# A third written order for the 791 pieces of an attention-and-experts kernel

## The chip, the cores and the metric

The kernel runs on one core of a Trainium2 chip. The metric is the device time of one execution in microseconds (us), as the median over several runs. The core has five engines that run side by side, each through its own instructions in order: PE (TensorE, matrix multiplication), DVE (VectorE), ACT (ScalarE), POOL (GpSimd) and SP (SyncE, which here only issues DMAs). An instruction that waits for another engine or for a DMA holds up all that stand behind it on its own engine. POOL issues DMAs too: the loads of the experts' weights, the scatters of token rows, and the writes of the output rows.

## The reference

A Nystrom attention over 8 batches of 8 heads (sequence 576, head dimension 64, 32 landmarks) gives 4608 tokens of 512 numbers. A mixture of 8 experts follows: each token goes to the expert with its greatest logit.

```python
q_lm = q.reshape(B, H, m, S // m, D).mean(axis=3)
k_lm = k.reshape(B, H, m, S // m, D).mean(axis=3)
A, Bm, C = sm(q, k_lm), sm(q_lm, k_lm), sm(q_lm, k)
Z = Bm.transpose(0, 1, 3, 2) / (norm_1(Bm) * norm_inf(Bm) + 1e-06)
for _ in range(6):
    Z = 2 * Z - Z @ Bm @ Z
x = rows_of(A @ Z @ C @ v)
...
e_idx = np.argmax(x @ w_gate, axis=1)
for e in range(E):
    mask = e_idx == e
    h = np.maximum(x[mask] @ w1[e], 0.0)
    out[mask] = gate_w[mask, None] * eom[mask, e, None] * (h @ w2[e])
```

`gate_w` is the softmax probability of the chosen expert and `eom` a sigmoid of `x @ w_output_gate`.

## The kernel before

The work is cut into eleven streams, Python generators that put instructions on the engines when they are advanced. A *piece* is what one advance emits, up to the generator's next `yield`. The string `ORDER` (line 20) holds one letter for each advance: line 950 walks along it, and each letter advances its stream by one piece. There are 791 pieces. So the string sets the order of the instructions on every engine at once, and no scheduler moves them afterwards. A stream that isn't ready (an event it needs hasn't been marked) answers "blocked", the letter then does nothing, and what is left at the string's end is done by a loop (line 952) that tries the streams in the order L G M T C A E N O R X. Pieces are numbered from 0 in their stream: X158 is the 159th piece of X.

The attention goes by 16 groups (4 heads of one batch), two to a batch, four to a pair of batches:

- L `loading` (line 752): q, k and v of a group are loaded by SP into parts of the weight buffer that aren't used yet (lines 216 and 220). A load needs that the group two before has used its place.
- G `summing` (line 223): POOL adds up q or k into landmarks, five instructions a piece (lines 228 to 232).
- M `marking` (line 235): ACT scales the landmarks.
- T `turning` (line 242): PE turns q and k, ACT copies them out of PSUM (lines 255, 256). Three pieces make q, three make k.
- C `softmax_c` (line 267) and A `softmax_a` (line 314): scores on PE, softmax on DVE and ACT.
- N `iteration` (line 339): the iteration for Z, eleven pieces a batch. Most are a few small matmuls (line 358) and one DVE instruction that waits for them (line 378), which the next piece waits for in turn.
- O `outputs` (line 403): five pieces a batch, each with eight matmuls (line 421), an ACT copy (425) and a DVE reduction (427). They use one PSUM buffer, the same one as the down projections of stream X.

Then the experts:

- R `directing` (line 838): for each pair of batches `routing` (line 449), which ends with nine scatters by POOL that sort the token rows by expert into `x_sorted` (line 528), and then the tables that say which rows a tile takes. Pair 0 is followed by a ranking of the experts by their token count (line 551). Of R's 73 pieces, R19 completes table 0, R55 to R68 are the routing of pair 3, R69 to R72 the last table (line 609): R70 computes how many tiles the ending has (line 627) and R72 the rows' addresses (line 655). In pair 3 SP also writes eight blocks of zero rows (line 522).
- E `bringing` (line 848): 32 loads, four for each expert, on POOL's queue (lines 141 and 144).
- X `working` (line 872): 26 *static* tiles of 128 rows in three stages. Stage 0 takes 8 tiles of the two largest experts, once table 0 is done; stage 1 takes 10 more, with pair 1's table; stage 2, the free tiles, takes 8 of any of the five largest, with pair 2's table. A tile is fetched by SP (lines 674 and 681; the first five of a stage in its first piece, each later one five tiles ahead), turned (line 695), multiplied up (707 or 718), in stage 2 turned again (726, copied by DVE at 728), and multiplied down (735) in two pieces that hold the output buffer. DVE scales (741) and POOL writes the rows out (743).

X0 is the first fetch of stage 0, X49 of stage 1, X110 of stage 2. In stage 2, X157 turns the hidden rows of the seventh tile (line 726). Piece X158 comes with a condition of its own:

```python
if stage == last - 1 and j == n - 2:
    yield from need("table", last)
    tables["which"] = which_ending()
    tc.switch_hint(tables["which"], len(ENDINGS), label="ending")
```

Every engine there reads the ending's number (`which_ending`, line 868), and X158 goes on with the first half of the last static tile. Behind all pieces stands a switch (line 965) over nine endings of different length. Its tiles are fetched by transposing DMAs (line 678), three ahead, and multiplied with an expert chosen by a register. In the profiled execution 12 tiles ran there.

While the attention runs, X's up projections use the two PSUM buffers of the transposes. When the last scores are done, stream A closes the attention's buffers (line 810), and from then on they have two of their own.

Of the kernel before, what the change touches and what calls it, by code (L numbers as in the profile page):

```python
# [17 lines left out]


ORDER = (  # L20
    "TTTGTTLTMCTGCTTACGCMCATTCTLMATCCTLAAAAGTCALCMTTCTCNGANLMCNATCGTLALCAACTGMCLTTANTLAMNCCTLGCANCNNLTCAN"
    "AANMGTCCTNNLTATAOLGAMCCNLGATOAACCTMAGNOCANTLTACTMNTANCLMNONNCACNLACNGOTTCGTMCANOALONTTATLOCCNOATNCGA"
    "AMNOCTRRCTCNARLRMNRTTTRLARCLNTNGCMNRRLGRRCRARAAACTCNCLTRTNLRNTAGOTLMATNRTEENRCRCONRCRNAGCNONTAMAACCG"
    "AEOTXTATNONLXCAALNCMGATTACCOTCAEAEXXOMXCOOLXTNMATXGAOLLRTRTNXERGLAXCXXMTXCNTRGCACRMTECCTAATNRARXMNCC"
    "XNXXNARRLTCENTAXCEXNXLTACTXLGTXARAALNLRGRETXXCNXMTNGCNAAXXONRXETXCNXNXAOLXANAOTNRAXNACOMNCGXTONCEXML"
    "TNALCRTXAGOCCXLXOTXXAMCXCAXGRETOCAOXXRCOTNNTTTXXERNXERCMNXXRRXXANREETXEXCNXRXARCRNXRRAXEMXEXREAETXXT"
    "CTXNXTRNRCTXRNXXXCLXAXEXCCEXXXXCRNCOXCEAAOAXXACXXXXXNEAXXAXXEXNOEXXEONXXNXXEOANRXXXXRXXNXXXRENXNXANE"
    "XXXXAXNXXXNAXXOXOOXOXXXOXRRRRRXRXXXXRXXRXXXXRRXXXRRRXXXXXXXXXRRXXXXXXRXXXXXXXRRXXXXXXXXXXXX"
)


# [972 lines left out]
```

## Time and profile before

| | us |
|---|---|
| median of 3 runs | 403.58 |
| the runs | 401.46 to 405.55 |
| the profiled execution, whole | 400.38 |
| its span, first to last instruction | 398.8 |
| PE busy | 330.1 |
| PE weight loads busy | 211.4 |
| DVE busy | 224.5 |
| POOL busy | 215.2 |
| ACT busy | 174.1 |

The profile is of one execution. The views used are: the page (busy time of each engine, and its share in 40 slices of the span); the view by windows (busy time in chosen stretches, with the clock granted to PE as a share of the full one, and the DMA engines' mean busy share, which comes out over 1 in some stretches); the view of waits (who waited for whom, in total, times, longest); and the timeline, whose rows give start, duration, engine, line, operation, output and inputs, and in brackets how long the engine idled before it and what ended that. PEld are weight loads, which run beside PE's matmuls. SPq and POOLq are the issuing sides of DMA queues. "issue" is an idle time for which the profile names no releaser. PE's busy time is modelled for pipelined matmuls.

### The profile page before, as it was taken

Reading aid. Unit: us, or ns where it says so; the run is one execution under the profiler, and the core shown is the slowest. Engines: PE = TensorE matmul, PEld = TensorE weight load, DVE = VectorE, ACT = ScalarE, POOL = GpSimd, SP = SyncE. Lnnn points to the kernel's source line nnn. Section 1 sums busy time; section 2 is a strip of 40 time slices with the busy share of each in tenths; the row PEclk is TensorE's granted clock in tenths of the full one; section 3 lists DMA queues with packets and bytes.
Section 4 is the critical chain, followed back from the end, with each engine's and each line's share of the span. In section 5 each row is a group of like instructions: output and inputs, shape, how many; then the busy total and the mean of one; then the engine's idle time right before and its main releaser. Section 6 shows DMA issues by size and latency. Waiting matters only on the chain. (4 is left out here: it accounts for less than half of the span.)

```text
span 398.8 us, 11916 instructions
## 1 busy us (share of the span) xinstructions
PE 330.1 (83%) x4503; PEld 211.4 (53%) x4532; DVE 224.5 (56%) x584; ACT 174.1 (44%) x413; POOL 215.2 (54%) x319
## 2 busy tenths in 40 slices
PE   2987878898679788989898999899989758799981
PEld 1555555665346655755566676576544424355540
DVE  5267776588587498655664844456527354234240
ACT  2565665767327655443555345342242112232320
POOL 2876966375885485488855565753312751022221
PEclk9999999999959999998999999999999989999997
DMA  8755555534748998984693999999940532323311
GB/s 265 225 181 189 172 179 181 129 105 137 265 81 186 292 220 227 172 256 99 136 252 79 221 240 244 211 218 228 255 135 27 200 132 58 97 73 100 96 54 46
DMA packets 46743, 66.44 MB, mean 167 GB/s; under 512 B 16208, under 2 KB 35024, under 8 KB 46672
## 3 DMA queue, kind: packets, MB, share of 16 engines
q0 software_dynamic: 17568, 30.98, 35.4%
q1 hardware_dynamic: 29104, 34.56, 29.8%
q8 instruction: 39, 0.64, 0.6%
q14 instruction: 32, 0.26, 0.2%
HBM read 65.35 MB, written 15.91 MB: 204 GB/s over the span
## 5 line engine op out<-in xcount | busy, mean ns | idle before, releaser
L743 POOL DMA_INDIRECT out_dram<-y,ic x38 | 39.1, 1030 | 102.6 <-DVE y L741 83.0
L735 PE MATMUL py<-W,hT 128*128 (+1 forms) x281 | 70.7, 382 | 6.5 <-DVE hT L728 4.4
L228 POOL TENSOR_TENSOR lms<-W 128x576 f32<-128x576 f32 x30 | 42.9, 1429 | 40.5 <-DMA W<-in_q_dram 39.4
L741 DVE TENSOR_SCALAR y<-py,ic 128x512 f32<-128x512 f32 x38 | 28.5, 750 | 62.5 <-PE py L735 46.2
L255 PE MATMUL tp<-ident,W 128*128 128x128 f32 x288 | 51.6, 301 | 12.7 <-ACT W L256 7.4
L256 ACT COPY W<-tp 128x512 f32<-128x512 f32 (+1 forms) x96 | 48.0, 517 | 29.5 <-PE tp L255 29.0
L721 ACT ACTIVATE h<-ph 128x512 bf16<-128x512 f32 x40 | 23.9, 598 | 64.7 <-PE ph L718 38.8
L735 PEld LDWEIGHTS <-hT 128*128 128x128 bf16 x304 | 29.2, 99 | 37.2 <-DVE hT L728 4.7
L255 PEld LDWEIGHTS tp<-ident,W 128*128 128x128 f32 x288 | 34.9, 150 | 23.3 <-ACT W L256 11.2
L528 POOL DMA_INDIRECT x_sorted<-row,r_slot x36 | 36.6, 1017 | 14.3 <-issue 5.2
L707 PE MATMUL ph<-xT,W 128*128 128x128 bf16 x576 | 38.1, 219 | 1.8 <-issue 1.0
L421 PE MATMUL po<-vbd,AT 64*128 64x160 f32 (+1 forms) x320 | 33.6, 326 | 5.1 <-DVE L L427 4.4
L707 PEld LDWEIGHTS <-W 128*128 128x128 bf16 x576 | 33.3, 98 | 5.8 <-issue 4.6
L427 DVE TENSOR_REDUCE L<-po 128x16 f32<-128x128 f32 (+1 forms) x40 | 11.6, 289 | 43.6 <-ACT row L425 43.6
L710 ACT ACTIVATE hT<-ph 128x512 bf16<-128x512 f32 x36 | 21.3, 597 | 33.5 <-PE ph L707 23.7
L425 ACT CAST row<-po 128x512 bf16<-128x512 f32 (+1 forms) x40 | 23.4, 586 | 24.5 <-PE po L421 20.2
L358 PE MATMUL pw<-WV 32*32 32x96 f32 (+1 forms) x768 | 26.9, 252 | 7.9 <-DVE WV L378 5.8
L264 PE MATMUL S<-W 64*32 64x288 f32 x512 | 27.0, 480 | 5.5 <-ACT BC L289 3.7
L421 PEld LDWEIGHTS po<-vbd,AT 64*128 64x128 f32 (+1 forms) x320 | 22.8, 178 | 13.1 <-DVE L L427 6.4
L229 POOL TENSOR_TENSOR lms<-lms 128x256 f32<-128x256 f32 x30 | 25.2, 839 | 2.4
L358 PEld LDWEIGHTS pw<-WV 32*32 32x32 f32 x768 | 15.9, 108 | 19.3 <-DVE WV L378 10.2
L718 PE MATMUL ph<-W,x 128*128 x95 | 22.4, 379 | 1.7 <-DVE y L741 1.3
(166 smaller groups left out, 539.0 us busy)
## 6 DMA issues: line engine op xcount, KB each, us to landing
W<-in_moe_w_dram POOLq DMA_DIRECT2D x32, 512.0 KB
W<-in_q_dram SPq DMA_DIRECT2D x16, 576.0 KB
W<-in_k_dram SPq DMA_DIRECT2D x16, 576.0 KB
W<-in_v_dram SPq DMA_DIRECT2D x16, 576.0 KB
x<-x_sorted SPq DMA_DIRECT2D x26, 128.0 KB
x_sorted<-zeros SPq DMA_DIRECT2D x9, 129.0 KB
ic<-x_sorted SPq DMA_DIRECT2D x38, 1.0 KB
out_dram<-y,ic POOLq DMA_INDIRECT x38
```

The source lines that it names most:

```text
L228: nc.gpsimd.tensor_tensor(s, t[:, :hg, :], t[:, hg:, :], op=OP.add)
L229: nc.gpsimd.tensor_tensor(s[:, 0:4, :], s[:, 0:4, :], s[:, 4:8, :], op=OP.add)
L255: nc.tensor.transpose(p[:, i, :], in_=tv[:, c0 + i] if c0 + i < hg else lm, identity=I128)
L256: nc.scalar.copy(tT[:, c0:c0 + n, :], p[:, :n, :])
L264: nc.tensor.matmul(p[hs, par, :hg * 32], lhsT=lhs[pr, hg, hs], rhs=cols(rhs[pr, :hg, hs]))
L358: nc.tensor.matmul(p[hs, gi, lo:32 + D], lhsT=cur[hs, gi, :32], rhs=cur[hs, gi, lo:])
L421: nc.tensor.matmul(po[ps, hp, gi * 2 * VC:(gi + 1) * 2 * VC], lhsT=ATs[gi][hs, 128 * c:128 * c + n], rhs=vbd[hs, gi].rearrange("p a b -> p ...
L528: i = nc.gpsimd.indirect_dma_start(out=xs, out_offset=bass.IndirectOffsetOnAxis(ap=slot[:, c:c + 1], axis=0), in_=rows[c], in_offset=None)
L707: nc.tensor.matmul(ph[:, 128 * i:128 * i + 128], lhsT=columns(t, dc * F + (half * FCH // 2 + i) * 128, 128), rhs=t["xT"][:, dc, :], start= ...
L735: nc.tensor.matmul(t["py"], lhsT=t["hT"][:, fc, :], rhs=columns(t, DCH * F + fc * HD, HD), start=(fc == 0), stop=(fc == FCH - 1))
L741: nc.vector.tensor_scalar(out=y, in0=t["py"], scalar1=t["coef"], scalar2=None, op0=OP.mult)
L743: i = nc.gpsimd.indirect_dma_start(out=out, out_offset=bass.IndirectOffsetOnAxis(ap=t["id"], axis=0), in_=y, in_offset=None, bounds_check= ...
```

## The change

Only the string is replaced, by another of 791 letters with the same number of each.

```diff
 ORDER = (
-    "TTTGTTLTMCTGCTTACGCMCATTCTLMATCCTLAAAAGTCALCMTTCTCNGANLMCNATCGTLALCAACTGMCLTTANTLAMNCCTLGCANCNNLTCAN"
+    "TTTTTLTGCCGMTTTMCACTCGTMATCTACTAAALGCCCAMLTTTCATACLLGNCMCTGLLNATAAGLNCATMTCNCCNALGTNMTANCATLCNTCALNA"
...
-    "XXXXAXNXXXNAXXOXOOXOXXXOXRRRRRXRXXXXRXXRXXXXRRXXXRRRXXXXXXXXXRRXXXXXXRXXXXXXXRRXXXXXXXXXXXX"
+    "NOAENXXNOXXXOXXOXXOXORRXXRRXARXRXXXRXXRXXXRXXXXXRRXRXRXXXERXRXXXXXEXXXXXXXXXXXXXRXXXRXXXXRX"
 )
```

Place of some events, counted in pieces from the start of the work:

| event | before | after |
|---|---|---|
| expert 0, 1, 2, 3, 4 fully issued | 331, 411, 496, 566, 590 | 311, 376, 411, 500, 574 |
| expert 5, 6, 7 fully issued | 626, 664, 699 | 665, 691, 766 |
| pair 0, 1, 2, 3 scattered | 255, 480, 612, 761 | 273, 461, 611, 758 |
| table 0, 1, 2, last | 284, 537, 691, 778 | 329, 504, 661, 781 |
| attention over, its buffers closed | 711 | 728 |

In the old string each letter does its piece. In the new one eight letters X near the end find X158 blocked, since the last table isn't done; R70, R71 and R72 then stand directly behind one another after X157, and the last eight pieces of X are done by the closing loop. In the old order R70 stands ahead of X148, and R71 and R72 ahead of X155.

What stands between the nine scatters of a pair on POOL's queue, in the two programs (s a scatter, y a write of output rows, G the five instructions of a landmark sum, E an expert load):

| pair | before | after |
|---|---|---|
| 0 | s s s s s s s s s G | s s G s s s s G s s s G |
| 1 | s s s s G s s E y G s s E y s G | s s s s y s s G s s y E s E G |
| 2 | s s E E s s E E y s s s s s y E E | s s s s s s y s s s y y E y E |
| 3 | s s s s s s s s y s y y y | s s s s y s s s s E s y E y y |

On SP's queue the first fetches of stage 0 stand, in the old order, ahead of v of group 10 and q, k and v of group 11; in the new one behind them. The outputs of pair 3, the routing of it (R55 to R63) and the free tiles keep about the places that they had relative to one another.

More of the change, by code (lines that the diff above doesn't have):

```diff
@@ L20 @@
 ORDER = (
-    "TTTGTTLTMCTGCTTACGCMCATTCTLMATCCTLAAAAGTCALCMTTCTCNGANLMCNATCGTLALCAACTGMCLTTANTLAMNCCTLGCANCNNLTCAN"
[L22 to L27, printed above, removed]
-    "XXXXAXNXXXNAXXOXOOXOXXXOXRRRRRXRXXXXRXXRXXXXRRXXXRRRXXXXXXXXXRRXXXXXXRXXXXXXXRRXXXXXXXXXXXX"
+    "TTTTTLTGCCGMTTTMCACTCGTMATCTACTAAALGCCCAMLTTTCATACLLGNCMCTGLLNATAAGLNCATMTCNCCNALGTNMTANCATLCNTCALNA"
+    "CANMACNTGTCNTTNOLNAMOCALCALANTOACGCTNCMCAGTTANTTMNCCLLLTANGATAOCMTAONCNGATTACGTMACNTLNCOLNCAOLANATCO"
+    "GCAATONACNMAORTTNRCTARGCMLNCTRNTRRAMNRRTRTLCNGCTANCLLRCTGLNALMNCCORNRGTRMRACARAAGTCATTCNRCRTTNCCONAE"
+    "NLECMONRAECECCATLONTNLREATLNORNGANOXMTONTAONXLOTGAXNACAXMXOCLXEXRAETARCXCAXXEMTGARXXARETNCXAXTECEAXT"
+    "TRRXXRXALNXECCXXLMXTRTNTGCRANRMRCNXNRCALXOGXACXTNRTXXAATNMXEXRXNAONCNEXXXCTRCGRXXNAOLTTXCXXAEXXMXCOL"
+    "EGLXRNTXLACNTXXNEMTGTXELXNCXXTCXNOGXXTOCLCOCAEMAATCOXXONXNXAXLNXXXTNAOXRXTEAEXXRCGRXXNRMXXRTERARRRRX"
+    "XCRRTXCMXRNRRCAXAXXTXTATRXAXXCNACXXTXRXCXNXCAXEXXNCCACNXCNXAORXXNEXEXNXNXEAXXXXNXNOXAXNOXNEEXAXENXAO"
+    "NOAENXXNOXXXOXXOXXOXORRXXRRXARXRXXXRXXRXXXRXXXXXRRXRXRXXXERXRXXXXXEXXXXXXXXXXXXXRXXXRXXXXRX"
 )
```

## The prediction

> **What bounds the kernel now.** First the page: how full TensorE is.
>
> ```profile
> span 398.8 us, 11916 instructions
> ## 1 busy us (share of the span) xinstructions
> PE 330.1 (83%) x4503; PEld 211.4 (53%) x4532; DVE 224.5 (56%) x584; ACT 174.1 (44%) x413; POOL 215.2 (54%) x319
> ```
>
> PE is the one full engine, and the change neither adds nor removes an instruction of the computation. So 330.1 us of PE work stay, and only the 68.7 us in which PE idles (398.8 - 330.1), and stretches at half clock, can change. The page's row of PE in tenths has two hollows behind the start, near 105 and 320 us. The view by windows, read next, measures these and two smaller ones like them:
>
> ```profile
> 104.00:110.00 6.00, 2.73 (x49) 1.52 (x34) 2.09 (x11) 1.03 (x4) 4.87 (x9) 1.00 0.53 196
> 110.00:122.00 12.00, 9.42 (x140) 5.98 (x140) 9.28 (x21) 3.16 (x8) 10.01 (x14) 0.57 0.53 96
> 174.00:178.00 4.00, 2.43 (x31) 1.45 (x33) 1.99 (x5) 1.21 (x3) 3.61 (x5) 1.00 0.88 336
> 178.00:184.00 6.00, 5.78 (x71) 3.21 (x64) 3.25 (x10) 1.75 (x5) 5.14 (x9) 0.72 0.13 43
> 248.00:256.00 8.00, 5.90 (x104) 4.23 (x104) 4.08 (x15) 2.98 (x9) 5.23 (x8) 1.00 0.98 244
> 312.00:325.00 13.00, 7.39 (x43) 3.45 (x43) 4.77 (x16) 1.79 (x3) 10.35 (x15) 1.00 0.46 163
> 325.00:330.00 5.00, 3.95 (x22) 2.07 (x21) 3.54 (x11) 1.23 (x3) 0.99 (x1) 0.66 0.27 105
> ```
>
> The columns are stretch, length, then PE, PEld, DVE, ACT and POOL busy, clock, DMA share, GB/s. PE, DVE and ACT are all slack at once, while POOL stays busy. What POOL does there, from its timeline:
>
> ```profile
> 96.88 1.63 POOL L528 DMA_INDIRECT x_sorted<-row,r_slot  x1 [0.44 <-POOL row L527]
> ...
> 109.55 0.97 POOL L528 DMA_INDIRECT x_sorted<-row,r_slot  x1 [0.28 <-issue]
> ...
> 170.77 1.07 POOL L528 DMA_INDIRECT x_sorted<-row,r_slot  x1 [0.32 <-POOL row L527]
> ...
> 175.25 0.97 POOL L528 DMA_INDIRECT x_sorted<-row,r_slot  x1 [0.28 <-POOL row L527]
> ...
> 245.32 1.04 POOL L528 DMA_INDIRECT x_sorted<-row,r_slot  x1 [0.28 <-POOL row L527]
> ...
> 254.75 0.99 POOL L743 DMA_INDIRECT out_dram<-y,ic  x1 [0.30 <-issue]
> ...
> 309.36 0.97 POOL L528 DMA_INDIRECT x_sorted<-row,r_slot  x1 [0.68 <-DVE xT L697]
> ...
> 326.76 0.99 POOL L743 DMA_INDIRECT out_dram<-y,ic  x1 [1.84 <-DVE y L741]
> ```
>
> These are runs of indirect DMAs with no other POOL work between: 9 for pair 0, 4 for pair 1, 6 for pair 2, and 12 for pair 3 (nine scatters, three outputs). Count a run's price as PE's idle time plus the part of its busy time that the lower clock takes. Pair 0: 6 - 2.73 = 3.3, 12 - 9.42 = 2.6, and 9.42 x (1 - 0.57) = 4.0, together 9.9 us. Pair 1: 1.6 + 0.2 + 5.78 x 0.28 = 3.4. Pair 2: 8 - 5.90 = 2.1. Pair 3: 5.6 + 1.1 + 3.95 x 0.34 = 8.0. Long runs cost most. The trace doesn't say why; I take the length of the run as the cause, and weigh another below.
>
> **The change, part by part.** It moves pieces only. At the end the letters aren't carried out as written: piece X158 needs the last table, so eight X letters do nothing, the last three R pieces (R70 to R72) come in one block behind X157, and the closing loop does the rest.
>
> *The end.* The work between the last outputs and the ending is the same. What moves is the table. Rows of before:
>
> ```profile
> 321.77 0.14 DVE L627 TENSOR_SCALAR ending<-more 1x1 int32<-1x1 int32 x1
> ...
> 322.92 0.19 DVE L634 TENSOR_SCALAR eo<-ef 128x43 int32<-128x43 f32 x1
> 327.94 0.16 DVE L639 TENSOR_SCALAR dd<-done 128x8 f32<-128x8 f32 x1
> ...
> 330.42 0.19 DVE L655 TENSOR_SCALAR bi<-bf 128x43 int32<-128x43 f32 x1
> 331.85 1.32 SPq L678 DMA_TRANSPOSE x<-x_sorted  x1
> 332.36 0.68 DVE L728 COPY hT<-pt 128x1024 bf16<-128x1024 bf16 x1
> 332.70 1.89 PE L718 MATMUL ph<-W,xT 128*128 x7 [0.60 <-DVE y L741]
> 341.02 1.89 PE L718 MATMUL ph<-W,x 128*128 x8 [1.28 <-DVE y L741]
> ```
>
> ```profile
> 331.85:334.00 2.15, 1.49 (x11) 0.75 (x10) 1.19 (x2) 0.24 (x1) 0.98 (x1) 1.00 0.28 61
> ```
>
> The ending's number was ready at 321.9, long before PE read it. Now R70 stands behind X157's copy, which ends at 333.0 on this clock. The number comes at 333.3, PE needs 0.6 to load it (its idle time before 332.70, taken as that load), and the matmuls of 332.70 start near 334.1: +1.4. Behind the waiting PE lie tile 7's matmuls and two down projections; ACT, POOL and SP wait on the same number with nothing else urgent. The block takes 1.5 (from just before 321.77 to 323.1) plus 2.7 (327.94 to 330.6), so the rows' addresses come at 337.2, not 330.6, and the first fetch at 338.5 (1.24 later, as before). Its 128 KB moved within 2.15 us (61 GB/s x 2.15 = 131 KB), so it lands near 341, inside 341.02 + 1.4. Ends: 0 if the DVE freed at 321 gives it back; +6.7 if the fetch needs the whole 9.2 us from 331.85 to 341.02. I take +2, near the low end because of the 2.15 us row, the rest for PE's clock after 2 us of idling.
>
> The last two expert loads, E30 and E31, now stand among pair 3's scatters. The last stage reads any expert, so it waits for them. They go out about 322 and 326, and a load lands in about 8.5 us (below): 335, before 341. Nothing.
>
> *The scatter runs.* In the new POOL order pair 0 has its scatters as 2, 4 and 3, with landmark sums between: like pair 1's run of four (3.4) in place of 9.9, so -6.5; ends -9.9 and 0; I take -5. Pair 1 goes from 4 to 7 in a row (4, an output, 2): between 3.4 and 9.9; I take +2; ends 0 and +6.5. Pair 2 loses the expert loads that broke it up: 6, an output, 3, two outputs, 12 in a row, as pair 3 has: 8.0 - 2.1 = +6; ends 0 and +8. Pair 3 is split by one load only: 0, ends -2 and +2. Together +3.
>
> *SyncE's queue.* Before, the first static tile's fetch stood ahead of the loads of group 11 and waited for table 0:
>
> ```profile
> SPq L671 <- DVE done L604: 13.7, 1, 13.7
> 134.42 1.39 POOL L228 TENSOR_TENSOR lms<-W 128x576 f32<-128x576 f32 x1 [8.53 <-DMA W<-in_q_dram]
> ```
>
> POOL waited 8.5 us for a late q load of group 11. Now the fetch stands behind group 11's loads, so that wait goes; late next is group 12, whose sum comes much later. PE hardly waited for it: -1, ends -2 and 0. But the first tile is now turned only about eight PE pieces behind table 0 (some 5 us: PE's 330.1 us lie on about 500 pieces), with those loads ahead of its fetch on the queue. Landing in 2.15 us, as above, costs nothing; landing in 8.5, after an issue 1.2 behind the table, costs about 5: I take +1, near the first, for its 128 KB.
>
> *Spacing on PE.*
>
> ```profile
> PE pw L358 <- DVE WV L378: 5.8, 9, 2.1
> ```
>
> Iteration steps with no other PE work between fall from 4 to 1, outputs with none from 3 to 1: 5 x 0.64 (5.8 over 9) = -3.2 at most, pricing an output's wait like an iteration's. Against it, static and output pieces, which share one PSUM buffer, stand closer from piece 500 on: +3 at most. I take -1. The first two free tiles now use the transposes' two buffers, because the attention ends 17 pieces later: +0.5, ends 0 and +1.2.
>
> The moves of the expert loads themselves cost nothing: all are issued well ahead of the matmuls that read them.
>
> Sum: 2 + 3 - 1 + 1 - 1 + 0.5 = +4.5. The profiled execution took 400.38 us, 3.2 less than the median of the runs shown, 403.58. So 404.9 on its own time, and 408.1 beside the median. For this kernel 1% (4.0 us) is what tells a change from none.
>
> **The clock.** The loss of clock from 110 to 122 us lasted: a mean of 0.57 there means some 10 us at half. [...]
>
> **Rivals.** *Faster: collisions, not runs.* In the stretch that led into the dearest stall the transfers were saturated:
>
> ```profile
> 102.00:104.00 2.00, 1.18 (x33) 0.66 (x37) 1.79 (x10) 1.65 (x3) 1.44 (x4) 1.00 1.02 404
> ```
>
> If a stall needs q and k loads in flight with scatters, pair 0's goes (-9.9), because its scatters are spread and the loads are ahead, and pair 2's doesn't come. Then 2 - 9.9 - 1 + 1 - 1 + 0.5 = -8.4: 395. It decides if pair 2's twelve cost less than 3 us. Against it: pair 3's run costs 8.0 at a share of 0.46. [...]
>
> *Much slower.* The fetch at the end needs its 9.2 us (+6.7 in place of 2) and pair 0 gives nothing back: +4.5 + 4.7 + 5 = +14: 418; one of the two alone: 413. For it: the fetch's landing isn't seen. Against it: the 61 GB/s row.
>
> *No change.* Pair 2 loses what pair 0 gains and the end costs 1.4: 403 to 405. The change does less than it says here, too: the last two expert loads are 65 and 67 places later, not sooner.
>
> **How the numbers follow.** Forecast 0.50, its own range 403 to 413: slower 0.32, same 0.18. Collisions 0.20, all faster. Much slower 0.18. No change 0.12. So faster 0.20, same 0.30, slower 0.50. The range leaves out the lower half of the fast case and the upper half of the slow one: 396 to 416.
>
> **What would show it.** The clock tenths full at 100 to 120 us; a new hollow with POOL full where pair 2 is scattered, near 250; PE waiting for L627 ahead of tile 7; the first DMA transposes behind PE's last static tile but one. Wrong if pair 2's twelve scatters pass with PE full, if the first transposed tile is used more than 3 us after PE's last static matmul, or if a stall comes in the first 90 us, where I count nothing.

## The result, and the profile after

The new order took 421.36 us (median of 4 runs, 417.23 to 423.30) against 404.56 of the old one beside it (401.46 to 410.58): a ratio of 1.041, 95% interval 1.031 to 1.050, so 17 us slower. The ratios in this document leave disturbed runs out, so they are not always the quotient of the medians shown, and the traces of e3, e7, e8 and e15 are of such runs.

The page of the new order's profiled execution (422.63 us, against 400.38 of the old one's): span, busy times, and the rows of PE and its clock in 40 slices.

```profile
span 420.9 us, 11913 instructions
...
PE 341.3 (81%) x4501; PEld 220.4 (52%) x4532; DVE 223.1 (53%) x584; ACT 175.1 (42%) x413; POOL 214.0 (51%) x319
...
PE   2888889877777899959899895998779766799991
...
PEclk9999999989889699969999997999999968999998
```

The work is the same, yet PE is busy 11.2 us longer (341.3 against 330.1) and idle 10.9 us longer (79.6 against 68.7). So half of the loss is matmuls that ran at a lower clock (mean granted clock 0.944 over the span, against 0.972), and half is waiting. The view by windows shows where (columns as in the prediction):

```profile
106.00:118.00 12.00, 9.30 (x135) 6.41 (x131) 6.81 (x22) 5.19 (x13) 9.89 (x18) 0.79 0.60 189
118.00:128.00 10.00, 7.45 (x127) 4.87 (x130) 4.15 (x15) 4.04 (x11) 7.96 (x12) 0.84 0.74 224
...
136.00:146.00 10.00, 9.10 (x81) 6.78 (x82) 4.96 (x20) 3.21 (x8) 2.66 (x5) 0.66 1.18 220
178.00:192.00 14.00, 9.07 (x89) 6.76 (x89) 6.80 (x13) 4.38 (x10) 11.13 (x17) 0.76 0.63 203
252.00:266.00 14.00, 9.37 (x89) 6.46 (x91) 5.16 (x13) 3.36 (x7) 11.15 (x17) 0.76 0.29 101
326.00:346.00 20.00, 13.48 (x75) 6.88 (x75) 6.34 (x16) 2.47 (x5) 14.47 (x22) 0.84 0.66 174
346.00:358.00 12.00, 8.41 (x37) 3.72 (x36) 5.29 (x18) 2.39 (x4) 1.40 (x2) 0.83 0.40 95
```

The first three are the stretch of pair 0's tables and first static tiles, the next three hold the scatters of pairs 1, 2 and 3, the last holds the last table. The hollow of the old order near 105 us did not go. It became a long shallow one, with PE partly idle or at a low clock from 106 to 146 us, and the hollows of pairs 1 and 2 deepened.

To put sizes to it, both traces can be read at equal *PE work*: PE's busy time, with what ran at half clock counted half (323 us in all by the old trace, 322 by the new; the records missing from both make some of that difference). By how much the new order is late at each point, worked out from the PE and clock records of the two traces:

| PE work done, us | 70 | 100 | 130 | 140 | 190 | 200 | 260 | 270 | 320 |
|---|---|---|---|---|---|---|---|---|---|
| new order late by, us | 0.3 | 6.1 | 5.4 | 9.5 | 9.6 | 15.3 | 20.4 | 24.4 | 25.4 |

So: +5 in the stretch of pair 0, +4 at pair 1's scatters (130 to 140), +6 at pair 2's (190 to 200), +5 spread over the outputs and static tiles of pair 3 (200 to 260), +4 at the last table (260 to 270), and little in the ending. The step from 260 to 270 also holds the last of pair 3's scatters and 6.8 us at half clock ahead of the table; of what the +5 before it is made, no run shows. These executions lie 22 us apart, a little more than the medians (17).

Where it is late at pair 2, the timeline shows it plainly. Three rows, each starting with start and duration:

```profile
254.70 0.96 POOL L528 DMA_INDIRECT x_sorted<-row,r_slot  x1 [0.28 <-issue]
...
258.44 0.60 ACT L710 ACTIVATE hT<-ph 128x512 bf16<-128x512 f32 x1 [4.64 <-remote]
...
259.09 1.97 PE L255 MATMUL tp<-ident,W 128*128 128x128 f32 x8 [3.94 <-issue]
```

PE idles 3.94 us and names no releaser, ACT idles 4.64 us until an event that the profile doesn't place ("remote"), and POOL goes on issuing a scatter every 1.4 us. This is the stall that the prediction expected of a long run. And the last table:

```profile
351.08 0.14 DVE L627 TENSOR_SCALAR ending<-more 1x1 int32<-1x1 int32 x1
...
353.43 0.59 PE L718 MATMUL ph<-W,xT 128*128 x1 [3.37 <-DVE wb L643]
...
354.81 0.18 DVE L655 TENSOR_SCALAR bi<-bf 128x43 int32<-128x43 f32 x1
...
356.22 1.53 SPq L678 DMA_TRANSPOSE x<-x_sorted  x1
...
363.36 1.89 PE L718 MATMUL ph<-W,x 128*128 x8 [1.24 <-DVE y L741]
```

PE waits 3.37 us for the table's block, and the first ending tile (363.36) waits for a scaled output and not for its fetch.

### The profile page after: what moved, and what is told of

It reads as the page before. It is cut to its first block, busy times and chain, and to the rows that moved or that the text cites. A ratio compares the mean times of both kernels' runs of the same rounds, so it can differ in the third digit from the quotient of the medians.

```text
span 420.9 us, 11913 instructions
## 1 busy us (share of the span) xinstructions
PE 341.3 (81%) x4501; PEld 220.4 (52%) x4532; DVE 223.1 (53%) x584; ACT 175.1 (42%) x413; POOL 214.0 (51%) x319
## 4 chain that ended last, share of the span: by engine, by line
PE 38%; DMA 15%; issue 14%; DVE 12%; POOL 8%; ACT 8%; another core or an unknown queue 2%; POOLq 1%; SPq 1%; ACTq 0%; DVEq 0%
DMA out_dram<-y,ic 9%; PE py L735 7%; PE tp L255 6%; PE ph L707 5%; PE po L421 5%; DMA W<-in_q_dram 4%; PE pw L358 4%; PE S L264 4%; ACT row L425 2%; PE pv L307 2%; POOL lms L228 2%; POOL out_dram L743 2%; POOL x_sorted L528 2%; PE tp L297 2%
## 5 line engine op out<-in xcount | busy, mean ns | idle before, releaser
L735 PE MATMUL py<-W,hT 128*128 (+1 forms) x278 | 73.6, 394 | 9.6 <-DVE hT L728 6.7
L255 PE MATMUL tp<-ident,W 128*128 128x128 f32 x288 | 55.3, 318 | 21.7 <-ACT W L256 6.9
L228 POOL TENSOR_TENSOR lms<-W 128x576 f32<-128x576 f32 x30 | 44.2, 1473 | 39.3 <-DMA W<-in_q_dram 38.2
L255 PEld LDWEIGHTS tp<-ident,W 128*128 128x128 f32 x288 | 38.0, 159 | 34.6 <-ACT W L256 9.8
L735 PEld LDWEIGHTS <-hT 128*128 128x128 bf16 x304 | 30.1, 101 | 40.2 <-DVE hT L728 7.4
L528 POOL DMA_INDIRECT x_sorted<-row,r_slot x36 | 35.4, 983 | 14.4 <-issue 7.0
L421 PE MATMUL po<-vbd,AT 64*128 64x160 f32 (+1 forms) x320 | 35.5, 342 | 7.5 <-DVE L L427 5.4
L425 ACT CAST row<-po 128x512 bf16<-128x512 f32 (+1 forms) x40 | 23.4, 585 | 33.6 <-PE po L421 28.2
L421 PEld LDWEIGHTS po<-vbd,AT 64*128 64x128 f32 (+1 forms) x320 | 24.4, 190 | 15.9 <-DVE L L427 8.2
L358 PE MATMUL pw<-WV 32*32 32x96 f32 (+1 forms) x768 | 25.9, 251 | 5.9 <-DVE WV L378 5.4
L229 POOL TENSOR_TENSOR lms<-lms 128x256 f32<-128x256 f32 x30 | 22.7, 758 | 2.4
```

Source lines behind the costliest of these rows:

```text
L228: nc.gpsimd.tensor_tensor(s, t[:, :hg, :], t[:, hg:, :], op=OP.add)
L255: nc.tensor.transpose(p[:, i, :], in_=tv[:, c0 + i] if c0 + i < hg else lm, identity=I128)
L358: nc.tensor.matmul(p[hs, gi, lo:32 + D], lhsT=cur[hs, gi, :32], rhs=cur[hs, gi, lo:])
L421: nc.tensor.matmul(po[ps, hp, gi * 2 * VC:(gi + 1) * 2 * VC], lhsT=ATs[gi][hs, 128 * c:128 * c + n], rhs=vbd[hs, gi].rearrange("p a b -> p ...
L425: nc.scalar.copy(rows[t].bitcast(BF16)[ps, :HD].rearrange("p (t gh d) -> p t gh d", t=2, d=D), pv[:, :, :, :D])
L528: i = nc.gpsimd.indirect_dma_start(out=xs, out_offset=bass.IndirectOffsetOnAxis(ap=slot[:, c:c + 1], axis=0), in_=rows[c], in_offset=None)
```

## The experiments

The runs fell on several chips of one type. On three of them the old order takes 380 to 385 us, on one 401, near the 405 of the first comparison. They are called the faster and the slower kind here; with so few chips that is a name for these times and no more. Each ratio is against the old order on the same chip.

| run | what | old order there, us | ratio | 95% interval |
|---|---|---|---|---|
| e5 | old order | 380.7 | one run, 382.56 us | |
| e6 | new order | 380.7 | 1.034 | 1.030 to 1.038 |
| e18 | new order | 384.8 | 1.030 | 1.022 to 1.039 |
| e2 | old, new end | 380.4 | 1.011 | 1.007 to 1.015 |
| e1 | new, old end | 380.4 | 1.032 | 1.025 to 1.040 |
| e14 | old, E30 and E31 late | 400.9 | 1.002 | 0.994 to 1.010 |
| e9 | new, E30 and E31 early | 381.7 | 1.034 | 1.027 to 1.042 |
| e10 | new, both of these undone | 381.7 | 1.029 | 1.022 to 1.036 |
| e4 | first 430 pieces new, rest old | 380.4 | 1.015 | 1.008 to 1.022 |
| e3 | first 430 old, rest new | 380.4 | 1.021 | 1.015 to 1.028 |
| e12 | old, pair 0's scatters 4 and 5 | 381.7 | 1.004 | 1.000 to 1.007 |
| e11 | new, ranking and table 0 early | 381.7 | 1.027 | 1.021 to 1.034 |
| e16 | old, ranking and table 0 late | 400.9 | 1.010 | 0.999 to 1.021 |
| e7 | old, pair 2 dense | 380.7 | 1.010 | 1.007 to 1.014 |
| e8 | new, pair 2 spread | 380.7 | 1.030 | 1.026 to 1.034 |
| e15 | pieces 431 to 661 new, else old | 400.9 | 1.044 | 1.031 to 1.056 |
| e13 | new, three parts undone | 400.9 | 1.032 | 1.023 to 1.042 |
| e17 | new, five parts undone | 384.8 | 1.008 | 0.999 to 1.016 |

Only the order of pieces differs. The diffs below are in pieces, along the sequence that the letters make. No run beat the old order.

### The two orders on another chip: e5 and e6

No edit. e5 gives the old order's trace there and e6 the new order's.

> The old order unchanged, for its trace on the chip of these runs: the kernel before took 380 us there against 404 in the first comparison. Both theories (the loss lies in stretches of scatters; the loss is one of clock) expect the same here: the ratio 1.00; the trace should show which of the hollows of before (105, 180, 250, 320 us) are there on this chip too.

> The new order unchanged on the same chip. If the parts add up (first 430 pieces 1.0146, the end 1.0107, some 1.5 per cent between them), 1.04 as in the first comparison; if the loss depends on the chip's slower transfers in the first comparison, under 1.03.

The new order is slower there too, by 1.034. That is between the two values expected, and its interval overlaps that of the first comparison. But the parts lie elsewhere. By the traces at equal PE work the new order is late by 0.2 us at 90, 6.6 at 100, 3.4 at 140, 6.6 at 160, 7.6 at 190, 7.2 at 200 and 9.9 at 260. Pair 2's run costs nothing. The windows of the same twelve us of program, from the first scatter of pair 2, first in the first comparison's trace, then in e6's:

```profile
250.00:262.00 12.00, 7.64 (x83) 5.14 (x77) 5.21 (x18) 2.88 (x7) 9.48 (x16) 0.83 0.40 119
```

```profile
239.80:251.80 12.00, 12.00 (x207) 8.57 (x210) 9.27 (x30) 5.68 (x13) 9.57 (x16) 1.00 0.39 115
```

POOL does the same in both, with the same DMA share, and on the second chip PE is full. So in the first comparison PE, DVE and ACT were slack beside pair 2's dense run (PE busy 7.64 of 12 us), and in e6, in the same place, PE was not (12.00 of 12; all traces are set side by side in the last section). The DMA views don't show slower transfers in the first comparison: the packets of the two large queues took 61.9 per cent of the new order's 420.9 us there and 67.5 of the 392.0 in e6, 261 and 265 us.

### The end: e2, e1, e9, e10, e14

e2, the old order with the new end, and e1, the new order with the old end (the same the other way round):

```diff
 X147
-R70
 X148
...
 X154
-R71 R72
 X155 X156 X157
+R70 R71 R72
 X158
```

> The old order with the new end: R70, R71 and R72 in one block between X157 and X158; all else as in the old order. Theory A (the block itself costs): +4 to +6 us, 1.010 to 1.015 of before, with a PE wait for L627 of over 2 us. The recorded estimate was +2 (1.005). Theory B: under 1 us (1.000 to 1.002).

> The new order with the old end: R70 ahead of X148, R71 and R72 ahead of X155; all else as in the new order. The two traces, set beside one another at equal PE work, part by another 4 us between the first pieces of pair 3's routing and the ending, and PE waits 3.4 us for the ending's number. Theory A (the block of the last table behind X157 costs this): the median falls by 4 to 6 us against the new order, so 1.025 to 1.031 of before; no wait of PE for L627 at 350 us, and the first ending tile no longer behind a late fetch. Theory B (the loss there is the clock's, or the work is only late because of pair 3's scatters, and the wait hides other waits): under 2 us, so 1.036 or more.

e2 cost 1.1 per cent, some 4 us. Its timeline:

```profile
313.17 0.14 DVE L627 TENSOR_SCALAR ending<-more 1x1 int32<-1x1 int32 x1
...
315.48 1.89 PE L718 MATMUL ph<-W,xT 128*128 x8 [3.33 <-DVE wb L643]
...
318.45 1.36 SPq L678 DMA_TRANSPOSE x<-x_sorted  x1
```

PE starts 2.2 us behind the end of L627, in every order with this end by 2.2 to 2.8 us. The profile names L643, which merely ends shortly before; PE's matmuls read nothing of `wb`. That the time goes to PE's load of the number is the likelier reading, and no run separates the two.

e1 should have given the same back, and gave nothing that can be told from zero (1.032 against 1.034 and 1.030 of the new order). What stands there in place of the wait:

```profile
319.81 0.19 DVE L655 TENSOR_SCALAR bi<-bf 128x43 int32<-128x43 f32 x1
...
319.95 1.01 POOL L528 DMA_INDIRECT x_sorted<-row,r_slot  x1 [0.28 <-POOL row L527]
...
327.53 1.35 SPq L678 DMA_TRANSPOSE x<-x_sorted  x1
...
333.92 3.57 PE L718 MATMUL ph<-W,x 128*128 x8 [6.01 <-DMA x<-x_sorted]
```

The addresses are there at 320.0, and the fetch goes out only at 327.5, 7.6 us behind the last scatter, and PE waits 6.01 us for the tile. In the old order (e5) the fetch follows by 2.95:

```profile
309.60 0.97 POOL L528 DMA_INDIRECT x_sorted<-row,r_slot  x1 [0.28 <-POOL row L527]
...
312.55 1.32 SPq L678 DMA_TRANSPOSE x<-x_sorted  x1
```

In the new order the 512 KB load E30 stands directly ahead of that last scatter on POOL's queue. e9 moves both late loads, alone; e10 moves them with the old end:

```diff
 X109
+E30
...
 X111
+E31
...
 X139
-E30
 R68 X140 R69
...
 X145
-E31
 X146
```

> The new order, with the expert loads E30 and E31 behind X109 and X111, ahead of pair 3's routing, in place of between and behind its scatters; the end as in the new order. In the trace of the new order with the old end the rows' addresses were ready at 319.8 and the fetch went out at 327.5, 7.6 us behind the last scatter; in the old order it went out 2.95 us behind the last scatter. Theory E (E30 stands ahead of the last scatter on POOL's queue and its bytes hold up that scatter's landing, on which the fetch waits): the fetch follows the last scatter by about 3 us where the table allows it, but here the table is late too (block behind X157), so 0 to -2 us against the new order (1.029 to 1.034 of before). Rival (the fetch waits on something else): no change, and still some 7.6 us.

> The new order with both: E30 and E31 early, and R70 to R72 as in the old order (ahead of X148 and of X155). Theory E with theory A (two causes in one place, either of which alone hides the other): 4 to 6 us less than the new order, 1.019 to 1.024 of before; PE's wait of 6 us for the fetched tile goes. Rival (the end costs nothing beside what stands before it): 1.030 to 1.034.

e9 changed nothing (1.034), as expected while the table is late anyway. In e10 the fetch follows the last scatter by 2.7 us and the wait for the tile is gone; the 1.29 us left are for a scaled output:

```profile
318.14 0.97 POOL L528 DMA_INDIRECT x_sorted<-row,r_slot  x1 [0.28 <-POOL row L527]
...
318.99 0.19 DVE L655 TENSOR_SCALAR bi<-bf 128x43 int32<-128x43 f32 x1
...
320.84 1.32 SPq L678 DMA_TRANSPOSE x<-x_sorted  x1
...
328.70 1.89 PE L718 MATMUL ph<-W,x 128*128 x8 [1.29 <-DVE y L741]
```

By the traces at equal PE work e10 gains 5.5 us on e6 between 260 and 270. Its ratio, 1.029, is only half a per cent under the new order's, inside the intervals, and short of the 1.019 to 1.024 expected. So the trace shows the fetch 2.7 us behind the last scatter with the loads early, in place of e1's 7.6; by what they hold it up no run shows, and the clocked runs don't settle what it is worth. e14 puts the late loads into the old order, alone:

```diff
 R54
-E30
 N83
...
 N85
-E31
 X103
...
 X141
+E30
 R68 R69 X142 X143 X144 X145
+E31
 X146
```

> The old order with E30 directly ahead of R68 (the last scatter) and E31 behind X145, as they stand in the new order; the table's pieces R70 to R72 stay where the old order has them. Theory E (the bytes of E30 hold up the last scatter's landing and with it the first fetch of the ending): the fetch 6 to 8 us behind the last scatter in place of 2.95, a wait of PE for x of 2 us or more, +2 to +6 us: 1.006 to 1.015. The recorded rival (the late loads cost nothing): 1.000 to 1.003.

1.002, nothing that can be told from zero. The last scatter was issued at 322.6 and the fetch went out at 331.2, 8.6 later. That is not the late load: on this kind of chip the fetch is 9.2 us behind the last scatter with early loads too (the first trace, e16), because the addresses come late, in e14 at 329.7. The tile was there when PE came to it. So beside a late table the late load costs nothing, as in e9, and it takes over when the table is mended, as in e1 (PE's wait of 6.01 us). On the faster kind the old order has its addresses 1 us behind the last scatter (e5); late loads alone were not tried there.

### Pair 0's stretch: e4, e3, e12, e11, e16

e4 and e3 cut the two orders at piece 430:

```diff
-order = old
+order = new[:430] + [p for p in old if p not in new[:430]]
```

e3 has `old` and `new` exchanged.

> The first 430 pieces in the new order, then all that is left in the old order. Theory C: +5 to +6 us, 1.012 to 1.016 of before. Rival: 1.000 to 1.005. If this one and the one with the first 430 old come out with losses that don't add up to the whole (about 16.8 us), the seam costs or gives something of its own.

> The first 430 pieces in the old order, then all that is left in the new order. Theory C (the stretch of pair 0's routing, its table and the first static tiles costs 5 to 6 us in the new order, by the traces at 130 us of PE work, and this stays lost): 1.025 to 1.03 of before, that is 5 to 6 us better than the new order. Rival (the early loss is given back by what follows, or is made by what follows): 1.036 to 1.042, as the new order.

The first part costs 1.5 per cent and the second 2.1, together what the whole costs. The first part is the one for which the prediction had -5 us. Its mechanism was tested by e12, which breaks pair 0's nine scatters of the old order:

```diff
 R9 R10 C44
-R11
 A39
-R12
 A40 A41 A42
...
-R13 R14
...
 A43 G17
+R11 R12 R13 R14
 O10
```

> The old order, with pair 0's scatters in runs of 4 and 5 in place of 9, a landmark sum (G17) between them: R11 to R14 behind G17; all else as in the old order. Theory G (the recorded one: a run's price grows with its length; 9 in a row 9.9 us, 4 in a row 3.4): 3 to 5 us faster, 0.987 to 0.992. Rival (the price is not the run's length but what PE has ready beside it, and the clock's windows): within 2 us of before or slower, 0.995 to 1.01.

1.004, no gain. A caution belongs to it: on this kind of chip the old order has much less of a hollow there. From 97 to 122 us PE is busy 20.2 of the 25 us in e5, its clock at 1.00 up to 110.8 and 0.85 behind; in the first trace of the old order it is busy 17.6 of the same 25 us, at 0.99 and 0.56. One step shows the difference, first in the first trace of the old order, then in e5:

```profile
104.30 0.25 PE L279 MATMUL S<-W 64*32 64x32 f32 x8
...
108.17 0.76 DVE L283 TENSOR_REDUCE nm<-S 128x1 f32<-128x576 f32 x1 [3.71 <-PE pw L358]
```

```profile
104.86 0.76 DVE L283 TENSOR_REDUCE nm<-S 128x1 f32<-128x576 f32 x1 [0.22 <-PE S L279]
```

The same scores (L279) are done at 104.55 in the first trace; DVE takes them up 3.6 us later there and at once in e5, while POOL issues its scatters in both. So e12 took the run apart where it stalled little. What breaking the run alone would give on the slower kind was not tried.

What costs there instead? The timeline of e6, first a row of POOL beside one of DVE, then a chain:

```profile
111.69 1.41 POOL L228 TENSOR_TENSOR lms<-W 128x576 f32<-128x576 f32 x1
...
111.85 1.34 DVE L560 TENSOR_TENSOR PM<-rank,ranks 128x64 f32<-128x64 f32 x1
...
115.10 0.74 DVE L283 TENSOR_REDUCE nm<-S 128x1 f32<-128x576 f32 x1
...
115.94 0.74 ACT L287 ACTIVATE eC<-S,nm 128x576 f32<-128x576 f32 x1 [4.26 <-DVE nm L283]
...
117.37 0.29 DVE L427 TENSOR_REDUCE L<-po 128x16 f32<-128x128 f32 x1 [1.52 <-ACT row L425]
...
117.97 0.86 PE L358 MATMUL pw<-WV 32*32 32x96 f32 x16 [2.21 <-DVE WV L378]
```

The ranking (L554 to L568, R15 and R16) stands on DVE ahead of a softmax step (L283). ACT waits 4.26 us for that step with the copy of an output (L425) queued behind it; DVE waits for the copy with the iteration's step (L378) queued behind that; PE waits 2.21 us for the step. e11 moves ranking and table up:

```diff
 R14
+R15
 A47
+R16
 A48 G19 T55
+R17
 C51 A49
+R18
 T56 T57
+R19
 C52 N36
-R15
...
```

> The new order, with ranking and table 0 moved up: R15 behind R14, R16 behind A47, R17 behind T55, R18 behind A49, R19 behind T57; all else as in the new order. Theory F (ranking and table stand on VectorE between the steps of the iteration and the outputs, some of them stretched beside POOL's landmark sums, so PE has short gaps of 1 to 2 us near 114 and 132 us and then runs 17 us at half clock): 4 to 6 us less than the new order, 1.018 to 1.024 of before, and under 10 us at half clock between 105 and 145 us. Rival (the outputs and the iteration wait for one another in any case, or the landmark sums between the scatters delay it): 0 to 2 us, 1.029 to 1.034.

e16 moves them down in the old order:

```diff
 N35
-R15
 T55
-E0 E1
 N36
-R16
+R15
 C48
-R17
 C49 O11 N37
-R18
+R16 E0 E1
 C50
-R19
 N38
+R17
 A45 G18 C51 N39
+R18
 O12 N40
+R19
 T56
```

> The old order, with ranking and table 0 some 15 pieces later, among the iteration's steps and the outputs, as the new order has them: R15 behind N36, R16 with E0 and E1 behind N37, R17 behind N38, R18 behind N39, R19 behind N40. Theory F: +2 to +4 us, 1.005 to 1.011, by more time at half clock between 105 and 145 us. Rival: 0.998 to 1.003.

Both moved the way theory F has it, and neither beyond its interval: 1.027 (from 1.034 and 1.030), between the two expectations, and 1.010 (0.999 to 1.021), as theory F has it. The windows from 110 to 146 us, of e6 and then e11:

```profile
110.00:146.00 36.00, 29.06 (x418) 20.82 (x406) 23.78 (x64) 14.95 (x36) 24.14 (x37) 0.76 0.87 190
```

```profile
110.00:146.00 36.00, 25.94 (x446) 18.46 (x445) 23.94 (x70) 17.05 (x41) 24.61 (x37) 0.91 0.84 189
```

The clock came up from 0.76 to 0.91, but PE's wait didn't go: one wait of 6.46 us for L378 took the place of three of 1.0 to 2.2.

```profile
117.69 0.86 PE L358 MATMUL pw<-WV 32*32 32x96 f32 x16 [6.46 <-DVE WV L378]
```

The moved pieces make that wait themselves: the rest of the ranking and the whole table (L566 to L604, two softmax steps between them) fill DVE from 111.4 to 117.4, and the iteration's step stands right behind. e16's trace is late by 3.4 us against e14's, of the same chip, at 130 us of PE work. So the chain is shown, and the ranking is in it wherever it stands among the iteration's steps; how much of the loss it is on the faster kind stays open.

### Pair 2's scatters: e7 and e8

```diff
 R46
+R47 R48 R49 R50
 A84 X55 E18 M29 X56 E19 X57
-R47
 E20
...
```

```diff
 R46 X69 X70 C85
-R47 R48
 T91 X71 C86
+R47
 M29 X72
-R49
 N71
-R50 R51
 C87 A83 X73
+R48
 A84 X74 X75 T92
+R49
 X76 T93 A85 T94
-R52
+R50 R51 R52
```

> The old order, with the scatters of pair 2 (R47 to R50) pulled up to stand directly behind R46, nine in a row with no expert load between; all else as in the old order. Theory D (a dense run of scatters stalls PE, here some 5 us, as the traces part at 190 to 200 us of PE work): +4 to +6 us, 1.010 to 1.016, with a half-clock stretch of 3.4 us or more near 240 us. Rival (a run stalls PE only where PE has little other work ready, or where its clock was lost anyway): under 2 us, below 1.005.

> The new order, with the scatters of pair 2 spread: R47 behind C86, R48 behind X73, R49 behind T92, R50 to R52 behind T94, so that the nine take about the stretch that they have in the old order; all else as in the new order. Theory D: 4 to 6 us less than the new order on this chip (1.025 to 1.03 if that is 1.04). Rival: within 2 us of it.

Making pair 2 dense cost the old order 1.0 per cent, the size that theory D has, but not in its way. In e7's trace PE is busy 14.8 of the 15 us from the first of the nine scatters on, as in e5, and the half clock comes at 254.7 and not near 240. What it loses, it loses some 15 us behind the run:

```profile
254.52 0.75 DVE L741 TENSOR_SCALAR y<-py,ic 128x512 f32<-128x512 f32 x1 [4.62 <-DMA out_dram<-y,ic]
...
255.33 0.91 PE L421 MATMUL po<-vbd,AT 64*128 64x160 f32 x4 [3.31 <-DVE y L741]
```

By the profile DVE waits there for a write of output rows, one of those that stand among the expert loads on POOL's queue, and PE for DVE. That is one trace, and no run tests it. Spreading pair 2 gave the new order 0.4 per cent, inside the intervals, as the rival has it. This agrees with e6: on this kind of chip the new order's dense run cost nothing in its trace, so there was nothing to give back. On the slower kind e13 (below) has the dense run, and stalls in it as the first trace does:

```profile
248.64 0.60 ACT L710 ACTIVATE hT<-ph 128x512 bf16<-128x512 f32 x1 [4.98 <-remote]
...
249.29 1.97 PE L255 MATMUL tp<-ident,W 128*128 128x128 f32 x8 [3.59 <-issue]
```

### All together: e13, e15, e17, e18

e13 is the new order with the moves of e11 and e10. e17 has these, those of e8, and pair 1 a little spread:

```diff
 R29 M23
-R30
 C69 N53
+R30
 X22 N54
-R31
 C70 A68 L34 X23 O20 G24
+R31
 X24
```

e15 is cut out of both orders, and e18 is the new order unchanged:

```diff
-order = old
+first = old[:430]
+middle = (first + [p for p in new if p not in first])[:661]
+order = middle + [p for p in old if p not in middle]
```

> The new order with all three parts undone that were tried alone: ranking and table 0 early (as in e11), E30 and E31 early, and the old end (both as in e10). If the parts add up: 1.034 less 0.007 less 0.005, that is 1.020 to 1.024 of before, and what is left (some 8 us) lies in the middle, between the first 430 pieces and the end. Rival (the repairs only shift the stalls, and the clock's windows with them): 1.027 or more.

> The first 430 pieces in the old order, those up to piece 661 in the new order (the scatters of pairs 1 and 2 and tables 1 and 2 among them), the rest in the old order. First 430 new cost 1.0146, first 430 old and all else new 1.0213. If the middle costs by itself (its scatter runs, the recorded terms +2 and +6): 1.008 to 1.014, and the end the rest. If the end makes nearly all of the later loss: 1.000 to 1.005.

> The new order with everything undone that a run or a trace has named: ranking and table 0 early, E30 and E31 early, the old end, pair 2's scatters spread (as in e8), and pair 1's spread a little (R30 behind N53, R31 behind G24). On the chip where before took 401 us, three of these left 1.032, and the traces still parted by 5.5 us at 190 to 200 us of PE work (pair 2's dense run) and by 3.4 us at 130 to 140 (pair 1's). If those two runs are the cause there: 1.008 to 1.015 on such a chip; on a chip where before takes 381 us, where the new order's trace showed no loss at pair 2: 1.015 to 1.022. If the rest is not in the named parts: no better than 1.03 on the first, 1.025 on the second.

> The new order unchanged, beside the one with five repairs on the same chip. On a chip where before takes about 401 us: 1.035 to 1.045 as in the first comparison, with stalls near 180, 255 and 335 us; on one where it takes 381: 1.032 to 1.036 as measured once. Were it under 1.025, the loss would not be the order's but the chip's.

e13 fell on the slower kind of chip: 1.032, above the sum of the parts and as the rival has it. By its trace the stretch of pair 0 is mended (late by 0.1 us against the old order's first trace at 130 us of PE work), and it is late by 3.5 at 140, 3.0 at 190, 8.1 at 200 and 11.0 at 320. Against e14, nearly the old order on the same chip, it is -0.5, 3.0, 2.5, 7.8 and 13.1. So the stretches of pair 1's and pair 2's scatters make some 8.5 of the 11 to 13. No run spread these two on this kind of chip.

e15 fell well outside both expectations: 1.044 from the middle alone, as much as the whole. Two cut orders may make stalls of their own at the seam, which no run parts off, so this says that the middle can cost that much on such a chip and no more.

e17 comes nearest to an answer: with the five parts undone the new order falls from 1.030 (e18, same chip) to 1.008, better than the 1.015 to 1.022 expected on such a chip. Medians 392.49 and 383.90 us, 8.6 us apart, some three quarters of the loss there. What is left lies inside the interval of no change. By the two traces at equal PE work e17 leads by 1.5 us at 130, 3.0 at 200, 2.9 at 260 and 8.3 at 270: more than half of the gain is the end, and none of it pair 2. This is the faster kind. For the 17 us of the first comparison the nearest run is e13, which leaves 1.032.

## Why the prediction was right or wrong

**What bounds the kernel.** Right: PE, and the loss came as idle time and half clock in about equal parts (10.9 and 11.2 us).

**The sum.** The direction was right and the size was not: +4.5 forecast, +17 measured, 5 us past the range's end. Its terms, against the first comparison's table at equal PE work:

| term | forecast | measured there |
|---|---|---|
| pair 0's stretch | -5 | +5 |
| pair 1's scatters | +2 | +4 |
| pair 2's scatters | +6 | +6 |
| spacing of outputs and static pieces on PE | -1 | +5 (from 200 to 260) |
| the end | +2 | +4 |
| SyncE's queue, first fetch, free tiles | +0.5 | not told apart |

**The step that failed** is "pair 0 has its scatters as 2, 4 and 3, with landmark sums between: like pair 1's run of four ... I take -5". It priced the stretch by the length of its runs of scatters. The shorter runs gave nothing back: from pair 0's first scatter to its last PE idles 4.8 to 5.0 us in the old place on the slower kind of chip (the first trace, e14, e16), 5.1 in the new order and 7.2 in e13. And it didn't ask what the iteration, outputs, ranking and table of that stretch would wait for, which the change had put among one another (e6's chain). With ranking and table early, e13's stretch comes out even with the old order (0.1 late against 5.4); with them late, the old order's is 3.4 late (e16). So of the 10 us between -5 and +5, about half go with the place of the ranking; the other half is a gain that never came, and why the shorter runs are no cheaper there stays open. The trace of the whole stretch (+5 at 130) and e4 (1.5 per cent for the first 430 pieces) say the same. The next largest is "I take -1" for the spacing. Where that term lies the new order lost 5, about half of it where pair 3's scatters begin (255 to 260); no run shows the cause. The two are 16 of the 20 us by which the terms are off.

**Pair 2** was right on the chip where it was forecast, in size and in form (POOL full, all engines slack, 250 to 262). It holds for that kind of chip: on the other, the same run passed with PE full. That its density is the cause rests on the traces, since no run took the run apart on that kind.

**The end** had the right mechanism and a term too small. The step is "PE needs 0.6 to load it": it took 2.2 us from the number to the matmul, and the step of the clock in which PE waited (350.0 to 353.4, PE busy 0.07 us) was followed by one at half clock (353.4 to 356.8, PE busy 3.17 us). The fetch was in time, as forecast, though the 2.15 us read as its landing were the length of a window: where the traces record it, the first fetch lands 2.7 us (e2) to 6.3 us (e10) behind its issue, and in the first comparison 7.1 us lay between fetch and tile. "The last two expert loads: Nothing" held alone (e14) and hid a wait of 6 us behind the late table (e1).

**The clock paragraph.** The 10 us at half rate in the old trace are three steps of 3.41 us, from 110.52 to 120.76 (see below). PE was busy for 42, 86 and 100 per cent of them, and the full clock came behind the first step that was busy throughout. The new order's stretch at 138.4, below, differs: PE was busy throughout its first step too (3.41 of 3.41 us), and the second ran at half as well.

**The rivals.** *Collisions* falls: pair 0's price didn't go, with the loads ahead. *Much slower* came nearest in time (418) by one of its two halves: pair 0 gave nothing back; the fetch's 9.2 us was not it, so that its time came near is luck. *No change* needed pair 0's gain.

**What would show it.** The wait for the number, the fetch behind the last static tile but one, and the hollow near 250 came; full clock tenths from 100 to 120 did not. Of the signs of being wrong none came on that kind of chip: the first transposed tile waited 1.24 us, and up to 90 us the new order was late by under 1. On the faster kind the first did: pair 2's scatters passed with PE full (e6).

## What to carry to other kernels

Price a new order stage by stage with all that is queued on each in-order engine there, not by the one pattern that stood out in the old trace: in e6 a ranking ahead of a softmax step, and an output's copy behind it, held PE for 2.2 us, and moving the ranking made it one wait of 6.5 (e11). When undoing one edit gives nothing, look for the wait that took its place before dropping the theory (e1 and e10). Before crediting a repair, see in the trace where its gain lies: most of e17's lies at the end. Measure a claim about stalls on the chip on which it was seen: the same 12 us were full on one chip and 64 per cent full on another.

## What the runs showed of the hardware

**Half clock lay on a grid of 3.413 us.** In all 20 traces every stretch of half clock behind the first 10 us starts on one grid of 3.413 us, fixed within an execution, and lasts one, two or three steps of it (but for the one at the program's end). Two such stretches of the first comparison's new order, by windows:

```profile
138.40:145.23 6.83, 6.83 (x62) 5.09 (x64) 2.50 (x9) 1.75 (x3) 2.23 (x3) 0.50 1.15 222
...
257.80:264.63 6.83, 5.54 (x32) 4.37 (x32) 1.05 (x2) 2.03 (x4) 5.24 (x9) 0.50 0.31 110
```

PE works through the first without a pause (6.83 of 6.83 us busy), at half rate. The step before tells more. Over all traces, from the first record of the clock to the stretch at the program's end, the steps at full clock sorted by PE's busy share in them, and what the next step ran at:

| busy share of a step | next at full clock | next at half |
|---|---|---|
| under 0.4 | 0 | 39 |
| 0.4 to 0.5 | 10 | 21 |
| 0.5 to 0.6 | 72 | 21 |
| over 0.6 | 1852 | 5 |

So in these traces a step in which PE was busy less than half (idle for over 1.7 us) was followed by one at half clock 60 times of 70, one with a share of 0.5 to 0.6 21 times of 93, and one above that 5 times of 1857. The new order spent 44.4 us at half clock in the first comparison and the old one 17.1 (the last stretch, at the end of the program, left out). Where the grid lies differs from run to run (in the first comparison, counted back to the start of the program, at 1.29 us in the old order's trace and at 1.83 in the new one's). That may be one reason why equal orders lose their clock in different places; no run tests it.

**Some small DVE operations beside POOL's sums took 1.3 to 2.1 us.** L560 took 1.34 us in e6 (rows above) against 0.22 in e5; L598 took 2.05 in e6, against 0.22 on average in e5; and in the first trace of the new order L582 took 2.04, against 0.17 on average in e5 and 0.21 in the first trace of the old order. Each lies beside POOL's L228 and ends within 0.1 us of it (L598 at 130.17, L228 at 130.14); two of them are recorded as starting first, so the rows don't show which came first, nor by what the one holds up the other, if it does.

**Two kinds of chips.** The same old order takes 381 and 401 us, and the order's price differs with it. How long PE idles from a pair's first scatter to its last, in all 20 traces:

| scatters | slower kind, us | faster kind, us |
|---|---|---|
| pair 2, in the old order's place (23 to 24 us) | 2.0 to 3.0 (3 traces) | 0.6 (4) |
| pair 2, dense (14 to 16 us) | 4.2 to 4.8 (3) | 0.0 to 0.2 (8) |
| pair 2, spread as in e8 (14.5 us) | none | 0.0 (2) |
| pair 3, all orders (14 to 15 us) | 3.0 to 6.5 (6) | 0.0 to 0.7 (14) |

On the slower kind PE idles beside every order's scatters and more beside the dense run; on the faster kind hardly at all. At pair 2's dense run the engines stopped together ("remote", "issue") in all three traces of the slower kind (first comparison, e13, e15) and in none of the eight of the faster one. The DMA view counts the packets of two queues that it calls instruction queues, 39 and 32 in an execution. In the first comparison's new order the last two ahead of that stall end at 251.7 and 253.0, after 0.3 and 1.1 us, and none lies in it (PE idles from 255.2 to 259.1). So none of these transfers is to be seen beside the stall there; what does stop the engines stays open.
